# Attention computed once in query-major form, and feed-forward blocks moved behind it

## The chip, the cores and the metric

The kernel runs on one core of one Trainium2 chip. The metric is the device time of one execution in microseconds (us), the median of three runs. PE is TensorE (its weight loads, which overlap its matmuls, are listed apart as PEld), DVE is VectorE, ACT is ScalarE, POOL is GpSimd, and SP is the queue that issues every DMA.

## What is computed

Rotary attention over 4 batches of 8 heads, with 576 positions of 64 numbers, feeds two feed-forward layers over the 2304 tokens. The weights arrive as 64-bit numbers.

```python
q_rot, k_rot = rotate(q), rotate(k)                      # (4, 8, 576, 64)
scores = (1 / np.sqrt(64)) * q_rot @ k_rot.transpose(0, 1, 3, 2)
attn = np.exp(scores - scores.max(-1, keepdims=True))
attn = attn / (attn.sum(-1, keepdims=True) + 1e-09)
x = (attn @ v).transpose(0, 2, 1, 3).reshape(2304, 512)
g = s * np.maximum(x @ w_in, 0) ** 2 + b                 # w_in 512 x 2048
x = g @ w_out                                            # w_out 2048 x 512
gate, val = x @ w_gate, x @ w_val                        # 512 x 1536 each
out = (gate / (1 + np.exp(-gate)) * val) @ w_out2        # w_out2 1536 x 512
```

## The kernel before

Every operation is first put into a list with its engine, an estimated duration, a priority and the buffers that it takes and frees (`Schedule`, `op`, `dma`). `sch.run()` then plays an event model through that list and emits each engine's instructions in the order that the model found. On the chip each engine works through its own fixed order and waits on semaphores. Products of 32-bit numbers are made from a high and a low part in the format that TensorE takes at full rate: a product in a feed-forward layer is three matmuls (`mm3`, L953 to L956: high by high, high by low, low by high).

*Attention.* Heads go in 16 pairs. `prep(p)` loads q and k of a pair, rotates them (15 operations on POOL), transposes them on TensorE (9 transposes, L504), splits them into high and low parts (`qkhi`, `qklo`) and spreads these by six or seven DMAs (L540) into the operand tiles `a`, `t`, `kh` and `ac`, of which there are two sets, one for even and one for odd pairs. A set is taken for the next pair but one when the last matmul that reads it, one of the transposed scores, is done (`opb0`, `opb1`).

`head(n)` computes the scores of one head twice. The first time they are query-major (L632: 10 tiles of 128 by 288, two matmuls each), only so that DVE can take each row's maximum (L634) and, in 20 of the heads, ACT the sum of exponentials (L637). The maxima are turned into a row by a TensorE transpose and written as two extra rows into `ac`, in most heads through a DMA to memory and one back (`c_d`). The second time the scores are key-major (L762: 10 tiles, two matmuls each), with the maximum already subtracted by the extra rows. ACT takes the exponentials, which are at once the operand of the product with v. In 20 heads the exponentials are split in two and multiplied with `[vh|vl]`, the two parts of v side by side (L831, L833: 18 matmuls of 288 columns). The other 12 heads, 11 in `PLAIN` and one in `BH`, use a 32-bit matmul (L784), which the trace records as two instructions.

*Feed-forward blocks between.* `block_a(j)` takes 256 of the first 1536 tokens through half of the first layer (8 of 16 chunks of 128 hidden units). Its instructions are laid between those of the attention as fast as batches of attention are finished, and its partial sums go to memory (`p_d`). The 16 weight tiles that it needs are loaded and decoded during attention (`weight`: one 512 KB DMA into one of two `raw` buffers, L335 to L346 to turn 64 into 32 bits, L364 and L371 for high and low part).

*Feed-forward after attention.* `block_b` takes 384 tokens at a time: two full blocks, then four half blocks, to which the partial sums are added. `block_2` then takes six blocks of 384 tokens through the second layer (L954 to L956 for gate and value, L1198 to L1200 for the last product, whose matmuls have 512 columns). Only when attention has left its memory (`switch`) do the other weight tiles get their place.

PSUM has eight banks: five for scores and transposes (`t`), one for the product with v (`v`), and one each for the feed-forward blocks' hidden units (`h`) and sums (`x2`).

The two passes over the scores are these lines of `head` (L631 to L634 and L761 to L763):

```python
for y, (lh, rh) in enumerate(((a, t), (ac, kh))):
    nc.tensor.matmul(ps[:, 0:HS], lh[:, q0:q0 + 128], rh[:, c0_ + hf * HS:c0_ + (hf + 1) * HS], start=y == 0, stop=y == 1)
def mx(i=i, hf=hf):
    nc.vector.tensor_reduce(out=st["nm"][:, hf, i:i + 1], in_=st["s", i, hf], axis=AX.X, op=ALU.max, negate=True)
...
for y, (w, m) in enumerate(((t, a), (kh, ac))):
    nc.tensor.matmul(
        ps[0:kn, 0:HS], w[:, c0_ + kc * 128:c0_ + kc * 128 + kn], m[:, c0_ + qh * HS:c0_ + (qh + 1) * HS], start=y == 0, stop=y == 1
    )
```

Of the kernel before, what the change touches and what calls it, by code (L numbers as in the profile page):

```python
# [181 lines left out]
def tile_attention_moe_moe(  # L182
# [22 lines left out]
    FA = F1 // 2  # L205
# [4 lines left out]
    UA = 256  # L210
    UB = 384
    NA = 1536
    LATE, LAST = 1 << 20, 1 << 21
    PLAIN = (0, 1, 2, 3, 4, 5, 6, 9, 10, 13, 17)
    XP0 = 100
    XL0 = "dve"
    BH = (7,)
    DX = 1
    EWA = 0
    EVA = 0  # L220
    LDA = 800
    E1P = ("apaa", "ppap", "apaa", "ppap", "ppap", "rpap", "ppap", "pprp", "appa", "ppap", "apaa", "ppap", "apaa", "ppap", "apaa", "apaa", "apaa", "apaa", "apaa", "apaa", "apaa", "apaa", "apaa", "ppap", "apaa", "ppap", "aaaa", "ppap", "ppap", "ppap", "apaa", "apaa")
    MULE = "pool"
    WARM = 40
    G2P = 1
    RLD = 0
    SOFF = {5: 8, 31: -3, 25: 5, 23: 8, 21: -5, 22: 8}
    TOFF = {9: -3, 15: -8, 29: -8, 26: -8}
    A0 = 5000
    AS = 20  # L230
    AR = 1.0
    AVP = 3
    CPR = 8
    EVP = 8
    STP = 16
    FASTC = 4
    LA = 0
    WP0 = 80
    WPS = 4
    GLA = ("pool", "act", "dve")  # L240
    XLA = "dve"
    GLB = ("dve", "dve", "dve")
    PREP = 24
    PREP1 = 20

    GA = 8
# [4 lines left out]
        "raw": 2, "dec": 2, "wa": 2 * FA, "x": 2, "vr": 2, "ry": 1, "hi": 1, "vh": 3, "opb0": 1, "opb1": 1, "sm": 3, "l": 3, "cr": 1, "e": 2, "ph": 4,  # L251
        "pl": 4, "xo": 2, "tmp": 2, "rb": 1, "t": 5, "v": 1, "x2": 1, "h": 1, "xh": 2, "ya": 2, "ga": GA, "ra": 1,
# [4 lines left out]
    wa_p = ctx.enter_context(tc.tile_pool(name="wa", bufs=2 * FA))  # L257
    raw_p = ctx.enter_context(tc.tile_pool(name="raw", bufs=2))
    dec_p = ctx.enter_context(tc.tile_pool(name="dec", bufs=2))
    moa = ExitStack()  # L260
    xh_p = moa.enter_context(tc.tile_pool(name="xh", bufs=2, side="right"))
    ya_p = moa.enter_context(tc.tile_pool(name="ya", bufs=2, side="right"))
    ra_p = moa.enter_context(tc.tile_pool(name="ra", bufs=1, side="right"))
    ga_p = moa.enter_context(tc.tile_pool(name="ga", bufs=GA, side="right"))
    ps_x = ctx.enter_context(tc.tile_pool(name="ps_x", bufs=1, space=PSUM))
    ps_h = ctx.enter_context(tc.tile_pool(name="ps_h", bufs=1, space=PSUM))

# [147 lines left out]
    for g in range(G):  # L415
# [3 lines left out]
        if g == 0:  # L419
            eye_op = dma(ident, eye, 65536, -99, after=rt_op)  # L420
# [19 lines left out]
    def prep(p):  # L440
# [96 lines left out]
        if p:  # L537
# [13 lines left out]
            if p > 1:  # L551
                acs.append(sp(ac[64:66, 0:2 * S], lambda: kh[66:68], pr + 6))
# [749 lines left out]
```

## Time and profile before

| | |
|---|---|
| median of 3 runs | 1277.96 us (1275.68 to 1284.71) |
| profiled execution | 1277.72 us, its span 1275.9 us |
| PE, DVE, ACT, POOL busy | 1211.0, 738.1, 576.8, 332.5 us |
| TensorE instructions | 7236 matmuls |
| mean granted TensorE clock | 0.979 of full speed |

A busy share is the share of time in which at least one instruction of the engine was under way. Matmuls overlap each other by more than half, so that the time that one costs in a stream is read from the starts of successive ones and not from its duration. [...]

### The profile page before, as it was taken

How to read it: one execution, taken by the hardware profiler on the slowest of the kernel's cores; microseconds unless marked ns; L12 is line 12 of the kernel's file. 1: busy time of each engine (PE TensorE's matmuls, PEld its weight loads, DVE VectorE, ACT ScalarE, POOL GpSimd, SP SyncE). 2: the span in 40 equal slices, each digit the busy share in tenths (PEclk: the TensorE clock that was granted, in tenths of full speed). 3: DMA queues.
4: the chain of work that ended last, by engine and by line, in shares of the span. 5: the costliest groups of instructions: out<-in, count | busy, mean ns of one | idle time of the engine just before them, and what ended most of it. 6: DMA issues, size and time to landing. Idle time of an engine off the chain costs nothing.

```text
span 1275.9 us, 20228 instructions
## 1 busy us (share of the span) xinstructions
PE 1211.0 (95%) x7236; PEld 1123.1 (88%) x7236; DVE 738.1 (58%) x1652; ACT 576.8 (45%) x1549; POOL 332.5 (26%) x474
## 2 busy tenths in 40 slices
PE   6998798899999999999999999999999999999998
PEld 5666577698888889999999999999999999999997
DVE  6766777677888878688878846941212121121211
ACT  3655476678888888644434312431212121121111
POOL 8566556664564433211111000100000000000000
PEclk7899799999999989999999999999999999999999
DMA  6776664545543433343535522610001010010000
GB/s 138 168 177 155 178 154 99 106 106 128 137 104 89 119 82 85 101 143 118 164 118 163 191 82 65 191 33 16 35 1 50 1 50 1 1 50 1 26 1 25
DMA packets 124993, 116.56 MB, mean 91 GB/s; under 512 B 66870, under 2 KB 109128, under 8 KB 124892
## 3 DMA queue, kind: packets, MB, share of 16 engines
q1 hardware_dynamic: 124892, 115.26, 33.7%
q8 instruction: 57, 0.93, 0.3%
q14 instruction: 44, 0.36, 0.1%
HBM read 71.02 MB, written 17.55 MB: 69 GB/s over the span
## 4 chain that ended last, share of the span: by engine, by line
PE 83%; DMA 6%; DVE 6%; ACT 2%; SPq 1%; issue 1%; POOL 0%; DVEq 0%; ACTq 0%; POOLq 0%
PE hb L956 11%; PE hb L954 11%; PE hb L955 11%; PE ps_s L632 6%; PE ps_st L762 5%; PE acc L1200 4%; PE acc L1199 4%; PE acc L1198 4%; PE ps_av L784 4%; PE acc L955 4%; PE acc L954 3%; PE acc L956 3%; DMA ac<-qkhi 3%; DVE nm L634 2%; DMA ac<-kh 2%; PE ps_av L831 2%
## 5 line engine op out<-in xcount | busy, mean ns | idle before, releaser
L956 PE MATMUL hb<-xh,w 128*128 128x384 f32 x832 | 279.8, 336 | 0.0
L954 PE MATMUL hb<-xh,w 128*128 128x384 f32 x832 | 279.7, 336 | 0.0
L955 PE MATMUL hb<-xl,w 128*128 128x384 f32 x832 | 279.5, 336 | 0.0
L1228 DVE TENSOR_TENSOR si<-hb,si 128x384 f32<-128x384 f32 x72 | 40.1, 557 | 281.1 <-PE hb L956 280.7
L954 PEld LDWEIGHTS hb<-xh,w 128*128 128x128 f32 x832 | 156.2, 188 | 3.0
L955 PEld LDWEIGHTS hb<-xl,w 128*128 128x128 f32 x832 | 156.2, 188 | 3.0
L956 PEld LDWEIGHTS hb<-xh,w 128*128 128x128 f32 x832 | 156.2, 188 | 0.0
L634 DVE TENSOR_REDUCE nm<-ps_s 128x1 f32<-128x288 f32 x320 | 134.7, 449 | 36.4 <-PE ps_s L632 33.8
L371 POOL TENSOR_TENSOR w<-dec,w 128x512 fp32r<-128x512 f32 x42 | 58.5, 1393 | 273.1 <-ACT w L364 265.8
L632 PE MATMUL ps_s<-t,a 128*128 128x288 f32 x320 | 110.4, 351 | 10.2 <-DVE cr L666 4.3
L1226 ACT ACTIVATE si<-hb 128x384 f32<-128x384 f32 x72 | 35.4, 492 | 186.0 <-PE hb L956 182.9
L632 PE MATMUL ps_s<-kh,ac 128*128 128x288 f32 x320 | 96.3, 306 | 19.1 <-DMA ac<-kh 9.9
L762 PE MATMUL ps_st<-a,t 128*128 128x288 f32 (+1 forms) x320 | 104.0, 330 | 4.2 <-DVE rr L730 2.5
L1230 ACT ACTIVATE uh<-si 128x384 fp32r<-128x384 f32 x72 | 37.8, 525 | 149.2 <-DVE si L1228 149.2
L637 ACT ACTIVATE ps_s<-ps_s,nm 128x288 f32<-128x288 f32 x200 | 94.6, 474 | 12.8 <-DVE nm L634 12.1
L762 PE MATMUL ps_st<-ac,kh 128*128 128x288 f32 (+1 forms) x320 | 95.0, 302 | 2.0 <-DMA ac<-c_d 1.4
L632 PEld LDWEIGHTS ps_s<-t,a 128*128 128x128 f32 x320 | 62.6, 196 | 27.2 <-DVE cr L666 5.0
L955 PE MATMUL acc<-gl,w 128*128 128x384 f32 x256 | 85.9, 336 | 0.0
L954 PE MATMUL acc<-gh,w 128*128 128x384 f32 x256 | 85.6, 334 | 0.0
L956 PE MATMUL acc<-gh,w 128*128 128x384 f32 x256 | 85.5, 334 | 0.0
L1200 PE MATMUL acc<-w,ul 128*128 128x512 f32 x216 | 85.0, 393 | 0.0
L1199 PE MATMUL acc<-w,uh 128*128 128x512 f32 x216 | 84.8, 392 | 0.0
(134 smaller groups left out, 2856.9 us busy)
## 6 DMA issues: line engine op xcount, KB each, us to landing
raw<-in_moe_w_out_dram SPq DMA_DIRECT2D x28, 512.0 KB
raw<-in_moe_w_in_dram SPq DMA_DIRECT2D x16, 512.0 KB
raw<-in_moe_w_gate_dram SPq DMA_DIRECT2D x12, 512.0 KB
raw<-in_moe_w_val_dram SPq DMA_DIRECT2D x12, 512.0 KB
x_d<-xo SPq DMA_DIRECT2D x16, 288.0 KB
y_d<-y SPq DMA_DIRECT2D x24, 192.0 KB
xl<-y_d SPq DMA_DIRECT2D x6, 768.0 KB
out_dram<-o SPq DMA_DIRECT2D x18, 256.0 KB
```

The source lines that it names most:

```text
L371: e.tensor_tensor(out=W[key][:, 1], in0=val, in1=W[key][:, 0].bitcast(F32), op=ALU.subtract)
L632: nc.tensor.matmul(ps[:, 0:HS], lh[:, q0:q0 + 128], rh[:, c0_ + hf * HS:c0_ + (hf + 1) * HS], start=y == 0, stop=y == 1)
L634: nc.vector.tensor_reduce(out=st["nm"][:, hf, i:i + 1], in_=st["s", i, hf], axis=AX.X, op=ALU.max, negate=True)
L637: nc.scalar.activation(out=ps, in_=ps, func=AF.Exp, bias=st["nm"][:, hf, i:i + 1], accum_out=st["l"][:, hf, i:i + 1])
L762: nc.tensor.matmul(ps[0:kn, 0:HS], w[:, c0_ + kc * 128:c0_ + kc * 128 + kn], m[:, c0_ + qh * HS:c0_ + (qh + 1) * HS], start=y == 0, stop=y ...
L784: nc.tensor.matmul(st["av", qh][0:2 * D if wide else D + 1, 0:HS], vv, st["e", key][0:kn], start=kc == 0, stop=kc == 4)
L954: nc.tensor.matmul(o, lh, rh, start=first, stop=False)
L955: nc.tensor.matmul(o, lh, rl, start=False, stop=False)
L956: nc.tensor.matmul(o, ll, rh, start=False, stop=last)
L1198: nc.tensor.matmul(o, uh[:, cs], w[:, 0], start=first, stop=False)
L1199: nc.tensor.matmul(o, uh[:, cs], w[:, 1], start=False, stop=False)
L1200: nc.tensor.matmul(o, ul[:, cs], w[:, 0], start=False, stop=last)
```

## The change

Attention is rewritten by pairs of heads (`pair`). The scores are computed once, query-major, for nine tiles of 128 queries (the fifth tile holds the last 64 queries of one head and the first 64 of the other): four matmuls of 288 columns per tile, eight for the fifth. They lie in a PSUM tile of two banks, of which there are two (`s`). DVE takes the maximum of 576 columns in one instruction, and ACT the exponential of 576 columns with its sum, into a tile in SBUF (`e`, 12 buffers). TensorE then transposes the exponentials: 45 transposes of 128 columns a pair, four to a bank of `t` (3 buffers). ACT copies each bank into a high part, DVE subtracts it for the low part, and the product with `[vh|vl]` uses 512 columns (18 matmuls a pair) or, for the tile that two heads share, 64 columns (another 18). All heads go this way; the 32-bit product, the extra rows of maxima and their DMAs are gone, and the tile `ac` with its spreading DMA too. `a` is now laid out with a gap of 64 columns and filled by four DMAs of half its length, `t` by two, and `kz`, which was `kh`, by one. An operand set is taken for the next pair but one when the last scores of its pair are done.

`block_a` and its partial sums are removed: no feed-forward block is laid between the attention. After it, `block_b` takes all 2304 tokens through the full first layer in blocks of 512, 512, 512, 384 and 384, and `block_2` takes the same blocks through the second. The first block's first matmul is ordered behind the last scores (`s_turns`). 12 weight tiles are loaded during attention, the other 20 of the first layer behind `switch`. Sums use the two `s` tiles, hidden units the banks of `t` and `v`.

```diff
-    UA = 256
-    UB = 384
-    NA = 1536
+    UBS = (512, 512, 512, 384, 384)
+    WA = 12
+    WB = 20
+    NE = 12
...
             ops = []
             for s0, s1, d0 in a_pieces(0, 2 * S):
                 n = s1 - s0
+                ops.append(sp(a[0:64, d0:d0 + n], lambda s0=s0, s1=s1: st["hi"][0:64, s0:s1], s0 == 0))
+                ops.append(sp(a[64:128, d0:d0 + n], lambda s0=s0, s1=s1: st["lo"][0:64, s0:s1]))
+            ops.append(sp(t[64:128], lambda: st["hi"][64:128]))
+            ops.append(sp(t[0:64], lambda: st["lo"][64:128]))
+            ops.append(sp(kz[0:64], lambda: st["hi"][64:128]))
...
+        for u in range(NU):
+            pr = base + 10 * u
...
+                for hf in range(2):
+                    todo = [(q0, k0 + hf * HS, m) for q0, k0 in terms for m in (t, kz)]
+                    for y, (q0, k0, m) in enumerate(todo):
+                        nc.tensor.matmul(ps[:, hf * 512:hf * 512 + HS], a[:, q0:q0 + 128], m[:, k0:k0 + HS], start=y == 0, stop=y == len(todo) - 1)
+
+            def mx(u=u):
+                nc.vector.tensor_reduce(out=st["nm"][:, u:u + 1], in_=st["s", u], axis=AX.XY, op=ALU.max, negate=True)
+
+            def ex(u=u):
+                st["e", u] = e_p.tile([128, S], F32, tag="e", name="e")
+                nc.scalar.activation(
+                    out=st["e", u].rearrange("p (f n) -> p f n", f=2), in_=st["s", u], func=AF.Exp, bias=st["nm"][:, u:u + 1], accum_out=st["l"][:, u:u + 1]
+                )
+
+            o = s_prev = op("pe", t_mm(HS, 4 * len(terms)), s_mm, pr, (*main, s_prev), (s_tok, l_tok) if u == 0 else (s_tok,), (opb,))
+            in_turn(o, s_turns)
+            o = op("dve", t_dve(S), mx, pr, (o,))
+            exps[u] = op("act", t_act(S, True, 1) + 0.09, ex, pr + 1, (o,), (e_tok[u],), (s_tok,))
...
+        def unit(name, srcs, rows, pr, chain, av):
...
+            def tr():
+                ps = st["pt", name] = ps_t.tile([128, 512], F32, tag="t", name="ps_t")
+                for z, (u, k0, m) in enumerate(srcs):
+                    nc.tensor.transpose(ps[0:rows, z * 128:z * 128 + 128], st["e", u][:, k0:k0 + rows], ident)
+
+            def hi():
+                st["ph", name] = ph_p.tile([128, 512], F32R, tag="ph", name="ph")
+                nc.scalar.activation(out=st["ph", name][0:rows, 0:n], in_=st["pt", name][0:rows, 0:n], func=AF.Copy)
+
+            def lo():
+                ph = st["ph", name]
...
+                nc.vector.tensor_tensor(out=dst, in0=st["pt", name][0:rows, 0:n], in1=ph[0:rows, 0:n].bitcast(F32), op=ALU.subtract)
...
+        def product(name, out_cols, cols, o, toks, j, kcs, pr, chain, v_tok, first, stop, acq):
+
+            def av():
+                if v_tok not in st:
+                    st[v_tok] = ps_v.tile([128, 512], F32, tag="v", name="ps_av")
+                ps = st[v_tok][:, out_cols]
+                for y, (kc, c) in enumerate(zip(kcs, cols)):
+                    vv = st["vh"][j][:, kc]
+                    last = stop and y == len(kcs) - 1
+                    nc.tensor.matmul(ps, vv, st["ph", name][:, c], start=first and y == 0, stop=last and ("pl", name) not in st)
+                    if ("pl", name) in st:
+                        nc.tensor.matmul(ps, vv, st["pl", name][:, c], start=False, stop=last)
...
     for p in range(NP):
-        prep(p)
-        head(2 * p)
-        head(2 * p + 1)
-    for z in range(2 * FA):
-        weight(("out" if z % 2 else "in", z // 2), ("wa",), WP0 + WPS * z, spread_op[0][0][1][0])
+        sts[p] = prep(p)
+    for p in range(NP):
+        ends += pair(p, sts[p])
     n_att = len(sch.ops)
-    for j in range(NA // UA):
-        block_a(j)
...
+    for z in range(WA):
+        weight(("out" if z % 2 else "in", z // 2), ("wa",), WP0 + WPS * z)
+    sw = op("sp", 0.0, switch, LATE - 1, [o for o in sch.ops[:n_att] if o not in ends])
...
-                hs.append(op("pe", t_mm(n, 3), fn, prio + step * rate, (outs[kk], W_op["in", f], *hs[-1:]), (h_tok,) if kk == 0 else (),
+                hs.append(op("pe", t_mm(n, 3), fn, prio + step * rate, (outs[kk], W_op["in", f], *(hs[-1:] or s_turns[-1:])), (h_tok,) if kk == 0 else (),
```

## Rows read from the trace of the kernel before

**Rows 1.** The page's forty slices: TensorE's busy tenths and granted clock.

```profile
PE   6998798899999999999999999999999999999998
PEclk7899799999999989999999999999999999999999
```

**Rows 2.** Windows by stage: length, each engine's busy time and count, clock, DMA.

```profile
0.00:22.00 22.00, 12.78 (x101) 11.14 (x102) 9.88 (x21) 7.67 (x14) 18.39 (x35) 0.77 0.74 165
22.00:150.00 128.00, 111.54 (x593) 82.36 (x592) 94.22 (x211) 65.86 (x162) 82.87 (x112) 0.94 0.69 164
...
250.00:531.60 281.60, 262.16 (x1956) 249.46 (x1957) 226.41 (x626) 229.98 (x763) 129.49 (x209) 0.98 0.42 101
...
555.00:825.00 270.00, 269.99 (x1572) 269.30 (x1571) 212.21 (x388) 100.80 (x192) 31.70 (x22) 1.00 0.44 138
825.00:1275.90 450.90, 445.79 (x2341) 417.72 (x2340) 104.65 (x185) 91.55 (x180) 3.95 (x3) 1.00 0.07 23
```

**Rows 3.** Chain that ended last, 0 to 555 us: shares, one piece.

```profile
by line: PE ps_s L632 12.7%; PE ps_st L762 11.2%; PE ps_av L784 8.7%; DMA ac<-qkhi 6.0%; DVE nm L634 3.9%; DMA ac<-kh 3.6%; PE ps_av L831 3.5%; PE ps_av L833 3.2%; PE x2a L954 2.9%; PE h L954 2.9%; DMA c_d<-cr 2.9%; PE h L956 2.8%; PE h L95
...
381.26 6.48 DMA ac<-qkhi
```

**Rows 4.** Timeline of TensorE in the second layer: start, duration, instruction.

```profile
1262.34 0.34 PE L954 MATMUL hb<-xh,w 128*128 128x384 f32 x1
...
1266.58 0.39 PE L1198 MATMUL acc<-w,uh 128*128 128x512 f32 x1
...
1270.43 0.39 PE L1200 MATMUL acc<-w,ul 128*128 128x512 f32 x1
```

**Rows 5.** Timeline of TensorE in attention, at full clock.

```profile
300.50 0.29 PE L762 MATMUL ps_st<-a,t 128*128 128x288 f32 x1
...
302.20 0.28 PE L954 MATMUL h<-xh,w 128*128 128x256 f32 x1
...
302.55 0.29 PE L762 MATMUL ps_st<-a,t 128*64 128x288 f32 x1
...
354.55 0.91 PE L504 MATMUL pst<-ident,x 128*128 128x128 f32 x6 [1.61 <-DVE rr L730]
355.39 0.40 PE L632 MATMUL ps_s<-t,a 128*128 128x288 f32 x1
```

**Rows 6.** Timeline of TensorE at the first scores, at half clock.

```profile
21.41 0.45 PE L632 MATMUL ps_s<-kh,ac 128*128 128x288 f32 x1
...
22.37 0.45 PE L632 MATMUL ps_s<-kh,ac 128*128 128x288 f32 x1
22.61 0.84 PE L504 MATMUL pst<-ident,x 128*128 128x128 f32 x3
23.11 0.59 PE L632 MATMUL ps_s<-t,a 128*128 128x288 f32 x1
```

**Rows 7.** Timeline of DVE: nine maxima in a stream, and what follows.

```profile
200.12 3.50 DVE L634 TENSOR_REDUCE nm<-ps_s 128x1 f32<-128x288 f32 x9
203.53 0.40 DVE L1010 TENSOR_SCALAR r<-r,sv,bv 128x256 f32<-128x256 f32 x1
```

**Rows 8.** Groups by line: count, busy us, mean ns of one, idle before.

```profile
L1228 DVE TENSOR_TENSOR si<-hb,si 128x384 f32<-128x384 f32 x72 | 40.1, 557 | 281.1 <-PE hb L956 280.7
L485 POOL TENSOR_TENSOR x<-x,rt 128x384 f32<-128x384 f32 x46 | 48.3, 1050 | 0.9
L1249 ACT ACTIVATE o<-acc 128x512 f32<-128x512 f32 x12 | 7.1, 595 | 14.2 <-PE acc L1200 12.0 <-DMA out_dram<-o 2.1
L1247 DVE COPY o<-acc 128x512 f32<-128x512 f32 x6 | 4.2, 692 | 12.6 <-PE acc L1200 12.6
```

**Rows 9.** The chain, 505 to 515 us: two exponentials with their sums.

```profile
507.85 0.96 ACT ps_s L637 x4
```

**Rows 10.** Timeline of ACT: first and last of 13 streamed weight tiles.

```profile
560.33 0.63 ACT L364 ACTIVATE w<-dec 128x512 fp32r<-128x512 f32 x1 [2.49 <-DVE dec L346]
...
614.21 0.63 ACT L364 ACTIVATE w<-dec 128x512 fp32r<-128x512 f32 x1 [2.83 <-DVE dec L346]
```

More of the change, by code (lines that the diff above doesn't have):

```diff
@@ new lines, in r0, with r1, r2, r3 @@
+        def r0():
+            nc.vector.tensor_scalar(out=st["l"], in0=st["l"], scalar1=1e-9, scalar2=None, op0=ALU.add)
+        def r1():
+            nc.vector.reciprocal(out=st["l"], in_=st["l"])
+        def r2():
+            st["pr"] = ps_t.tile([128, 512], F32, tag="t", name="psr")
+            nc.tensor.transpose(st["pr"][0:NU, 0:128], st["l"], ident)
+        def r3():
+            st["rr"] = cr_p.tile([NU, 128], F32, tag="cr", name="rr")
+            nc.vector.tensor_copy(st["rr"], st["pr"][0:NU, 0:128])
@@ new lines, in pair @@
+        for j in range(2):
+            us = range(QA) if j == 0 else range(QA + 1, NU)
+            v_tok, tmp = Token("v"), Token("tmp")
+            chain = None
+            for kc in range(5):
+                pr = base + TA + TB * j + 9 * kc
+                name = (j, kc)
+                rows = 128 if kc < 4 else 64
+                o, toks = unit(name, [(u, kc * 128, 128) for u in us], rows, pr, None, None)
+                full = slice(0, 512)
+                chain = product(name, full, [full], o, toks, j, [kc], pr + AVP, chain, v_tok, kc == 0, kc == 4, kc == 0)
+            o = lower(512, (chain,), pr + 1, v_tok, tmp, j == 0)
+            evict(slice(0, 512), slice(64 * j, 64 * j + 512), j, o, pr + 1, v_tok, tmp)
@@ new lines, in pair @@
+        pr = base + TA + 2 * TB
+        o4, toks4 = unit("r", [(QA, kc * 128, 128) for kc in range(4)], 128, pr, None, None)
+        o5, toks5 = unit("rt", [(QA, 512, 128)], 64, pr + 1, None, None)
+        v_tok, tmp = Token("v"), Token("tmp")
+        chain, lasts = None, []
+        for j in range(2):
+            oc = slice(64 * j, 64 * j + 64)
+            chain = product("r", oc, [slice(128 * kc + 64 * j, 128 * kc + 64 * j + 64) for kc in range(4)], o4, toks4, j, range(4), pr + AVP, chain, v_tok, True, False, j == 0)
+            chain = product("rt", oc, [oc], o5, toks5, j, [4], pr + AVP, chain, v_tok, False, True, False)
@@ new lines, in pair @@
+        o = lower(128, (chain,), pr + AVP + 1, v_tok, tmp, False)
+        for j in range(2):
+            evict(slice(64 * j, 64 * j + 64), slice(512, S) if j == 0 else slice(0, 64), j, o, pr + AVP + 1, v_tok, tmp)
+        mul = op("pool", t_pool(S), lambda: nc.gpsimd.tensor_tensor(out=st["xo"], in0=st["xo"], in1=st["rb"], op=ALU.mult),
+                 pr + 20, (*evs, rb_op), (), (rb_tok,))
+        pp = p % (H // 2)
+        x_store[b].append(sch.dma(294912, lambda: nc.sync.dma_start(out=x_d[b][pp * 128:(pp + 1) * 128, :], in_=st["xo"]),
+                                  pr + 20, (mul,), (), (xo_tok,)))
@@ L1181, in block_2 @@
         nt = UB // 128
-        acc_toks = tuple(Token("acc") for _ in range(nt))
+        a_toks = (Token("s"), Token("s"))
+        acc_toks = (a_toks[0], a_toks[0], a_toks[1], a_toks[1])
         step = 0
@@ L1192, in fn @@
                     if first and c == 0:
-                        st["acc"] = [late["acc"].tile([128, 512], F32, tag="a", name="acc2") for _ in range(nt)]
+                        st["acc"] = []
+                        for _ in range(2):
+                            t = ps_s.tile([128, 1024], F32, tag="s", name="acc2")
+                            st["acc"] += [t[:, 0:512], t[:, 512:1024]]
                     w = W["out2", f]
```

733 lines of the change are left out of this document (203 added, 530 removed).

## The prediction, made before the change was run

> **What bounds the kernel now.** I read the page's slices first: TensorE is busy in every slice, solidly from slice 18 on, and before that with gaps in which its granted clock dips [rows 1]. So there are two kernels in one, and windows by stage separate them [rows 2]. From 555 us on TensorE is busy in 716 of 721 us at full clock: nothing but fewer or cheaper matmuls shortens that part. Before 555 us it holds attention and the early feed-forward blocks, and no engine is full: from 22 to 150 us TensorE is busy 87% and DVE 74% at a mean clock of 0.94; from 250 to 531.6 us 93% and 80%. The chain of waits says what is lost there [rows 3]: beside TensorE's own lines it holds 6.0% + 3.6% of 555 us, 53 us, in DMAs that spread a pair's operands (one piece is shown, 6.48 us), 2.9% in the row of maxima going through memory, and 3.9% in the maxima.
>
> **The feed-forward work, term by term.** Durations of matmuls overlap, so a price is the distance of starts. In the second layer 24 matmuls of 384 columns take 1266.58 − 1262.34 = 4.24 us, 0.177 each, and 17 of 512 columns take 3.85 us, 0.227 each [rows 4]. Among attention, 288 columns cost 0.131 (13 in 1.70 us) and 256 cost 0.117 (3 in 0.35 us) [rows 5].
> Before: `block_a` is 6 blocks of 8 chunks of 24 matmuls, 1152 × 0.117 = 135 us, and the rest is the 721 us from 555 on, of which the last 5 are eviction and the store; together 851 us.
> After: the first layer is 3 × 384 matmuls of 512 columns and 2 × 384 of 384: 1152 × 0.227 + 768 × 0.177 = 397 us. The second is 3 × 432 of 512, 2 × 288 of 384 and 2 × 108 of 512: 1512 × 0.227 + 576 × 0.177 = 445 us. Sum 842, take 843. Wider blocks save 8 us, no more; the fate of the change lies in attention.
>
> **What attention costs now.** 555 − 22 us of start − 135 us of `block_a` leaves 398 us for 16 pairs, 24.9 us a pair.
>
> **What a pair costs after, engine by engine.**
> TensorE: the scores are 40 matmuls of 288 columns, 5.2 us. Transposes are 45 for the exponentials and 9 for q and k; six took 0.84 us before the next matmul [rows 5], 0.14 each, and three 0.50 us at half clock [rows 6], which would be 0.083 at full clock. I take 0.11, as the ends are equally near, for 5.9 us (4.5 to 7.6). The product with v is 18 × 0.227 = 4.1 us. The 18 matmuls of 64 columns occur nowhere; between a proportional share of 288 columns (0.03) and a full such matmul (0.131) I take the 0.11 of a transpose: 2.0 us (0.5 to 2.4). Sum 17.2 us (14.3 to 19.3). The second pass over the scores and the 32-bit products that this replaces were 40 matmuls of 288 columns and more a pair, so that TensorE saves little: transposing is not much cheaper than computing again.
> DVE: nine maxima of 288 columns start to start take 3.41 us, 0.38 each [rows 7]. From 384 to 512 columns a duration grows from 557 to 692 ns [rows 8], 1.05 ns a column; so I estimate 0.68 for 576 columns, 0.615 for 512, 0.48 for 384 and 0.14 for 64. A pair has 9 maxima (6.1), 11 low parts (6.8) and a short one (0.2), evictions (2 × 0.615 + 2 × 0.14 = 1.5), three low parts of q and k (1.5) and small things (0.4): 16.5 us. Decoding 12 weights in 16 pairs adds some 1.2. Sum 17.7 us.
> ACT: two exponentials of 288 columns with their sums take 0.96 us in a stream [rows 9], so 0.48 each, and at 0.8 ns a column 0.71 for 576. A copy of 512 lasts 0.595 [rows 8], in a stream about 0.5. 9 × 0.71 + 11 × 0.5 + 1.2 for evictions + 1.4 for q and k + 0.8 for weights = 15.3 us.
> POOL: rotation at 1.05 us for 384 columns [rows 8], three times that and four halves of some 0.6, 10.4 us; splitting v, the multiply and the weights at the same 2.7 ns a column up to 6 more: at most 17.
>
> So four engines come out within 3 us of one another, DVE in front with 17.7 and TensorE beside it. How near a pair comes to 17.7 us depends on how well the fixed orders mesh. The trace has TensorE, the bound of its stages, at 0.87 and 0.93 busy [rows 2], the second with feed-forward matmuls to fill holes. I take 0.85, below both, because here two engines have to be full at once: 17.7 / 0.85 = 20.8, say 21 us. The ends are 0.95 (18.6 us) and DVE's own 0.74 of 22 to 150 us (24 us).
>
> **Where the stalls go.** The spreading DMAs keep their size (seven issues a pair on SP; one of 288 KB, that of `ac`, is gone, and two of `a` are halved into four), but the operand set is released after the last scores of its pair, not after a second pass. The next spread then has the other pair's scores, about 20 us, to land in, against pieces of about 6.5 us [rows 3]. I cost them at nothing; if SP is held up by a DMA queued in front of them (the store of 1 / sum and its broadcast, which wait for the pair's end), they are back at 53 us in the whole. The row of maxima, its transposes and its trips through memory are gone. What is late next is DVE: two `s` tiles, each held through 0.53 us of matmuls, 0.7 of maximum and 0.7 of exponential, and a maximum queued behind a low part holds up scores, exponentials and later transposes alike. `v` has one bank, and no product can start until ACT and DVE have emptied it.
>
> **The handover.** 13 weight tiles are finished 12 × 4.49 us apart [rows 10]. Before, 16 tiles had to come while the first late block ran. Now the first block (384 × 0.227 = 87 us) finds 12 and must get 20: 20 × 4.5 = 90 us, with some 8 us of head for the first. Its last chunk wants its weight at 82 us, and gets it at 91. I take a stall of 8 us, between 0 (if loading starts earlier than the block) and 20 (if it starts behind the last pair's evictions). The second layer's tiles have the last first-layer block and their own first block to come in, 36 tiles in some 165 us; no stall.
>
> **The sum.** Start until the first scores 22 (the same preparation [rows 2, 6]), 16 × 21 = 336, feed-forward 843, weights 8, last eviction and store 5: a span of 1214, and 2 outside it as in the profiled execution (1277.72 over 1275.9, which also stands within 0.3 us of the median): **1216 us**. Against before: 62 from the pairs, 8 from feed-forward, less 8 of stall. Everything but the pairs is 880, so the change breaks even at (1278 − 880) / 16 = 24.9 us a pair.
>
> **The rivals.**
> *Nearly saturated engines.* If the orders mesh at 0.95, a pair takes 18.6 us: 1178. For it: two pairs are in flight at different steps, with 12 buffers for exponentials. Against: one bank for `v`, two for scores, and no engine but TensorE passes 0.82 in the stages with attention [rows 2].
> *A latency-bound loop of scores.* DVE stays at 0.74 as from 22 to 150 us, 24 us a pair: 1264. For it: three engines follow one another in each tile and nothing fills TensorE's holes now. Against: in that stage the spreading DMAs are part of the loss.
> *TensorE at half clock.* This is the one that ends slower. While feed-forward blocks filled the holes from 250 us on, the mean clock was 0.98; in the stages without or nearly without them 0.77 and 0.94 [rows 2], after TensorE had waited. At half clock 288 columns cost 0.24 and a transpose 0.167 [rows 6]; with 512 columns at 0.43 and 64 at 0.167 a pair needs 9.6 + 9.0 + 7.7 + 3.0 = 29.3 us of TensorE, and 34 us with its waits. If half the pairs run so, a pair averages 27.5 us: 1320. It decides from 0.3 of the pairs on, where the average passes 24.9. Against: TensorE was kept at full clock through most of 22 to 150 us while it waited 13% of the time, and with 17.2 of 21 us it is about as busy here.
> [...]
>
> **How the numbers follow.** My forecast (20 to 22.5 us a pair, 1195 to 1245) has 0.54; saturated engines 0.16 (about 1178); the latency-bound loop 0.17 (1245 to 1290); half clock in a good part of the pairs 0.13 (above 1290). A measurement of this kernel cannot tell less than about 1% from no change, that is 1265 to 1291. Faster takes the first two and about half of the third: 0.79. The rest of the third is the same, 0.08. Slower 0.13. A range of 1170 to 1285 leaves out 0.05 below and some 0.14 above; it holds the bounds of the small matmuls and transposes (±2 us a pair where TensorE leads) and of the weight stall.
>
> **What the profile after would show.** Right: the last scores at about 355 us, and TensorE busy all the time behind that; DVE at some 0.85 until then, with the maximum and the low part as its two largest groups, near 750 and 690 ns in duration; no spreading DMA among the chain's first entries; clock at 1.00 but for the first 25 us; 384 matmuls of 512 columns in the first block with a gap of a few us near its end. Wrong: half-level stretches in the clock row within attention; TensorE waiting for DMA at each pair's first scores; DVE below 0.75, with waits in circles between scores, maximum and exponential; or a first block well over 100 us, its matmuls waiting for ACT's weight tiles.

## The result, and the profile after

The changed kernel takes **1243.63 us** in the median (1241.40 to 1244.78), against 1278.38 for the kernel before on the same chip: a ratio of 0.9719, with a 95% interval of 0.9681 to 0.9758. The forecast was 1216 us in a range of 1170 to 1285. The direction and the range hold; the time is 27.6 us longer than forecast.

The page of the changed kernel: span, TensorE, DVE and the granted clock in forty slices, to be laid beside [rows 1].

```profile
span 1239.6 us, 16562 instructions
...
PE   5788889998999989999999999999999999999998
...
DVE  5899989887988989334344388871311211221211
...
PEclk7999989999999999999999999999999999999999
```

Attention is now a stage of its own. It ends in slice 12 (a slice is 31 us). DVE's digits stay between 7 and 9 from slice 2 to slice 16, because behind attention DVE decodes weights beside the first feed-forward block, and then fall to 3; before, TensorE had feed-forward matmuls among attention up to slice 17. Windows by stage, cut at the first and the last maximum of the scores (columns as in [rows 2]):

```profile
0.00:22.20 22.20, 11.37 (x97) 9.96 (x97) 8.26 (x19) 6.60 (x13) 16.03 (x31) 0.80 0.70 161
22.20:364.70 342.50, 303.83 (x2024) 260.83 (x2025) 302.30 (x518) 262.93 (x587) 222.45 (x301) 0.97 0.62 147
364.70:1239.60 874.90, 860.16 (x4066) 740.94 (x4064) 383.52 (x617) 220.16 (x392) 43.86 (x29) 1.00 0.17 55
```

The middle row is the 16 pairs, but for what follows the last maximum: 342.5 us, **21.4 us a pair**. DVE is busy in 0.88 of it, TensorE in 0.89, ACT in 0.77, POOL in 0.65: as the sum had it, four engines close together with DVE and TensorE in front. The same measure of the kernel before, from its first maximum at 20.5 us to its last at 509.2, is 488.7 us, 30.5 us a pair, with 106 of the 135 us of `block_a` inside (895 of its 1138 recorded matmuls).

The groups by line in the changed kernel answer the durations that were worked out from [rows 7, 8, 9] (columns: busy us, mean ns of one, idle before and what ended it).

```profile
L582 ACT ACTIVATE e<-ps_s,nm 128x576 f32<-128x576 f32 x144 | 106.5, 740 | 29.8 <-DVE nm L578 28.3
...
L634 PE MATMUL ps_t<-ident,e 128*128 128x128 f32 (+1 forms) x720 | 107.2, 277 | 8.2 <-DVE qklo L485 4.4 <-ACT e L582 1.8 <-DVE pl L647 1.7
L578 DVE TENSOR_REDUCE nm<-ps_s 128x1 f32<-128x576 f32 x144 | 106.5, 749 | 10.8 <-PE ps_s L575 9.1
...
L647 DVE TENSOR_TENSOR pl<-ps_t,ph 128x512 fp32r<-128x512 f32 x144 | 96.9, 683 | 10.9 <-ACT ph L638 9.9
```

Maximum and low part are DVE's two largest groups in this stage, at 749 and 683 ns (foretold: near 750 and 690). TensorE's new instructions are priced by their starts, in its timeline among the pairs:

```profile
300.45 1.04 PE L634 MATMUL ps_t<-ident,e 128*128 128x128 f32 x8
301.25 0.38 PE L575 MATMUL ps_s<-t,a 128*128 128x288 f32 x1
...
302.66 0.30 PE L665 MATMUL ps_av<-ph,vh 128*128 128x64 f32 x1 [0.64 <-DVE xo L677]
...
304.69 0.38 PE L575 MATMUL ps_s<-t,a 128*128 128x288 f32 x1
```

Eight transposes take 0.80 us to the next start, 0.10 each; the 18 matmuls of 64 columns take 2.03 us, 0.11 each. Both had been set at 0.11, the second between 0.03 and 0.131 with no row of its own.

The chain of waits from 0 to 364.7 us ([rows 3] are its counterpart) shows no single owner, and the spread is still in it:

```profile
by line: PE ps_s L575 11.3%; PE ps_t L634 8.8%; DMA kz<-qkhi 8.6%; PE ps_av L665 8.4%; PE ps_av L667 6.9%; DVE nm L578 6.2%; issue 5.4%; SPq L510 3.8%; DVE pl L647 3.7%; ACT e L582 3.3%; DMA vr<-in_v_dram 3.2%; DVE qklo L485 3.2%; DVE xo L6
...
39.62 6.78 DMA kz<-qkhi
```

Two places behind the last maximum cost TensorE time. Near the end of the first feed-forward block the timeline of the changed kernel shows this:

```profile
437.39 0.50 PE L761 MATMUL hb<-xh,w 128*128 128x512 f32 x1 [0.94 <-ACT w L333]
437.41 1.28 POOL L340 TENSOR_TENSOR w<-dec,w 128x512 fp32r<-128x512 f32 x1 [5.38 <-ACT w L333]
...
437.44 1.53 DVE L824 TENSOR_SCALAR gh<-r,bv 128x512 fp32r<-128x512 f32 x1
...
438.75 0.50 PE L763 MATMUL hb<-xh,w 128*128 128x512 f32 x1 [0.63 <-POOL w L340]
...
527.78 0.49 DVE L824 TENSOR_SCALAR gh<-r,bv 128x512 fp32r<-128x512 f32 x1
```

TensorE waits for a weight's high part from ACT and then for its low part from POOL. DVE's `gh` lasts 1.53 us beside POOL's low part, and 0.49 us ninety microseconds later without it. The same pair of instructions appears in the last first-layer block, where the second layer's weights are decoded:

```profile
739.55 1.74 POOL L340 TENSOR_TENSOR w<-dec,w 128x512 fp32r<-128x512 f32 x1 [7.36 <-ACT w L333]
...
740.06 1.45 DVE L824 TENSOR_SCALAR gh<-r,bv 128x384 fp32r<-128x384 f32 x1
...
742.69 0.45 PE L762 MATMUL acc<-gl,w 128*128 128x384 f32 x1 [0.69 <-DVE gl L829]
```

### The profile page after: what moved, and what is told of

Its sections match the earlier page's. It is cut to its first block, busy times and chain, and to the rows that moved or that the text cites. A ratio compares the mean times of both kernels' runs of the same rounds, so it can differ in the third digit from the quotient of the medians.

```text
span 1239.6 us, 16562 instructions
## 1 busy us (share of the span) xinstructions
PE 1175.4 (95%) x6184; PEld 1011.7 (82%) x6184; DVE 694.1 (56%) x1150; ACT 489.7 (40%) x991; POOL 282.3 (23%) x360
## 4 chain that ended last, share of the span: by engine, by line
PE 74%; DVE 10%; DMA 7%; ACT 3%; SPq 3%; issue 2%; POOL 1%; ACTq 0%; DVEq 0%; POOLq 0%
PE hb L761 12%; PE hb L763 12%; PE hb L762 12%; PE acc L762 4%; PE acc L763 4%; PE acc L761 4%; PE acc L952 4%; PE acc L954 4%; PE acc L953 4%; PE ps_s L575 3%; PE ps_t L634 3%; PE ps_av L665 3%; DMA kz<-qkhi 3%; PE ps_av L667 2%; DVE nm L578 2%
## 5 line engine op out<-in xcount | busy, mean ns | idle before, releaser
L761 PE MATMUL hb<-xh,w 128*128 128x512 f32 (+1 forms) x800 | 296.7, 371 | 0.9 <-ACT w L333 0.9
L763 PE MATMUL hb<-xh,w 128*128 128x512 f32 (+1 forms) x800 | 296.3, 370 | 0.6 <-POOL w L340 0.6
L762 PE MATMUL hb<-xl,w 128*128 128x512 f32 (+1 forms) x800 | 295.8, 370 | 0.0
L761 PE MATMUL acc<-gh,w 128*128 128x512 f32 (+1 forms) x320 | 118.8, 371 | 3.8 <-DVE gh L824 3.8
L762 PE MATMUL acc<-gl,w 128*128 128x512 f32 (+1 forms) x320 | 119.3, 373 | 3.3 <-DVE gl L829 3.2
L575 PE MATMUL ps_s<-t,a 128*128 128x288 f32 x320 | 103.5, 340 | 18.1 <-ACT e L582 16.5
L665 PE MATMUL ps_av<-ph,vh 128*128 128x512 f32 (+1 forms) x320 | 106.8, 362 | 12.2 <-DVE xo L677 7.8
L582 ACT ACTIVATE e<-ps_s,nm 128x576 f32<-128x576 f32 x144 | 106.5, 740 | 29.8 <-DVE nm L578 28.3
L763 PE MATMUL acc<-gh,w 128*128 128x512 f32 (+1 forms) x320 | 118.2, 369 | 0.0
L638 ACT ACTIVATE ph<-ps_t 128x512 fp32r<-128x512 f32 (+1 forms) x192 | 104.1, 566 | 28.9 <-PE ps_t L634 27.7
L634 PE MATMUL ps_t<-ident,e 128*128 128x128 f32 (+1 forms) x720 | 107.2, 277 | 8.2 <-DVE qklo L485 4.4
L578 DVE TENSOR_REDUCE nm<-ps_s 128x1 f32<-128x576 f32 x144 | 106.5, 749 | 10.8 <-PE ps_s L575 9.1
L647 DVE TENSOR_TENSOR pl<-ps_t,ph 128x512 fp32r<-128x512 f32 x144 | 96.9, 683 | 10.9 <-ACT ph L638 9.9
```

Of the source, the lines that this page charges most:

```text
L575: nc.tensor.matmul(ps[:, hf * 512:hf * 512 + HS], a[:, q0:q0 + 128], m[:, k0:k0 + HS], start=y == 0, stop=y == len(todo) - 1)
L578: nc.vector.tensor_reduce(out=st["nm"][:, u:u + 1], in_=st["s", u], axis=AX.XY, op=ALU.max, negate=True)
L582: nc.scalar.activation(out=st["e", u].rearrange("p (f n) -> p f n", f=2), in_=st["s", u], func=AF.Exp, bias=st["nm"][:, u:u + 1], accum_ou ...
L634: nc.tensor.transpose(ps[0:rows, z * 128:z * 128 + 128], st["e", u][:, k0:k0 + rows], ident)
L638: nc.scalar.activation(out=st["ph", name][0:rows, 0:n], in_=st["pt", name][0:rows, 0:n], func=AF.Copy)
L647: nc.vector.tensor_tensor(out=dst, in0=st["pt", name][0:rows, 0:n], in1=ph[0:rows, 0:n].bitcast(F32), op=ALU.subtract)
```

## The experiments

Four theories were to be told apart; all concern what sets the 21.4 us of a pair. **A**, the prediction's own: DVE is in front, at 17.7 us, with TensorE just behind. **B**: the loop of one score tile (matmuls, maximum, exponential, two tiles in turn) sets the pace by its latency. **T**: TensorE is the bound. **D**: the DMAs that spread the operands, costed at nothing, hold the pairs up. Beside these stand the questions of what the un-laid feed-forward blocks were worth in the kernel before, and of what the weights cost behind attention.

All ratios are against the kernel before on the same chip, with 95% intervals. The stage is the time from the start of the first maximum of the scores to the end of the last in the profiled execution, and over 16 it is the pace of a pair.

| kernel | median us | ratio | stage us | us a pair |
|---|---|---|---|---|
| the change | 1243.63 | 0.9719 [0.9681, 0.9758] | 342.5 | 21.4 |
| e8_start (pairs untouched) | 1244.86 | 0.9712 [0.9675, 0.9749] | 348.1 | 21.8 |
| e10_low_dve (pairs untouched) | 1234.71 | 0.9657 [0.9615, 0.9699] | 346.4 | 21.6 |
| e1_spread | 1235.31 | 0.9643 [0.9613, 0.9672] | 336.9 | 21.1 |
| e2_low | 1236.37 | 0.9667 [0.9620, 0.9714] | 339.5 | 21.2 |
| e3_max | 1235.31 | 0.9655 [0.9601, 0.9708] | 339.2 | 21.2 |
| e4_scores | 1240.34 | 0.9689 [0.9650, 0.9728] | 341.7 | 21.4 |
| e7_all (low parts, maxima, scores) | 1226.79 | 0.9571 [0.9542, 0.9600] | 326.3 | 20.4 |
| e11_all_spread (e7 and spreads) | 1208.42 | 0.9427 [0.9398, 0.9455] | 311.3 | 19.5 |
| e13_all_act (e11 and ACT's high part) | 1196.80 | 0.9339 [0.9323, 0.9356] | 300.6 | 18.8 |
| e9_v2 | 1267.72 | 0.9887 [0.9851, 0.9923] | 361.7 | 22.6 |
| e12_wa14 | 1243.13 | 0.9702 [0.9679, 0.9725] | 345.6 | 21.6 |
| e5_unlaid | 1384.71 | 1.0805 [1.0769, 1.0840] | 466.5 | 29.2 |

The first three rows have the same pairs, and their stages lie between 342.5 and 348.1 us with a mean of 345.7. They come in the order of TensorE's mean granted clock in the profiled execution: 0.986 in the change, 0.983 in e10_low_dve, 0.977 in e8_start. A difference of 3 us from their mean therefore says nothing, and cuts are measured against the mean.

### One suspect at a time

**The spreading DMAs.** From the third pair on, each piece is cut to 32 columns.

```diff
+            n_sp = lambda o: o.shape[1] if p < 2 else 32
-  dma_start(out=o, in_=i())
+  dma_start(out=o[:, 0:n_sp(o)], in_=i()[:, 0:n_sp(o)])
```

> The changed kernel (1243.6 us) with the seven spreading DMAs of every pair from the third on cut to 32 columns each, so that the scores of those pairs are made of left-over operands; every issue and wait stays. The chain of waits of the changed kernel holds 7.9% of its first 400 us, 32 us, in these DMAs. Theory A (DVE's and TensorE's own work sets the pair, and the chain passes through the DMAs only because they are issued as late as they may): 1235 to 1244. Rival D (the spread is the wait that paces the pairs): 1205 to 1218.

1235.31 us, and a stage 9 us below the mean of the untouched ones. Its interval lies just below that of the change: 8 to 10 us in all, half a microsecond a pair. That is the lower end of A's range and far from D's 1205 to 1218. D is a part, and a small one while the rest stands.

**DVE's low parts**, 64 columns of 512, TensorE's work kept by reading those 64 again and again.

```diff
-  tensor_tensor(out=dst, in0=pt[0:rows, 0:n], in1=ph[0:rows, 0:n], op=subtract)
+  w = n if tail else 64
+  tensor_tensor(out=dst[:, 0:w], in0=pt[0:rows, 0:w], in1=ph[0:rows, 0:w], op=subtract)
```

> The changed kernel with DVE's low part of the exponentials computed for 64 of 512 columns, and the matmuls on it reading those 64 columns eight times, so that the low part is wrong and TensorE's work is the same: 9 times 0.47 = 4.2 us of DVE less in a pair. Theory A (DVE's total of some 17.7 us a pair is in front, TensorE's 17.2 right behind it): a pair falls from 21.8 to about 20.3 us, the run to 1215 to 1225. Rival B (the two score tiles, held through scores, maximum and exponential, pace the pair): 1235 or more, since the low part is not in that loop. Rival T (TensorE alone is the bound): 1238 to 1244.

**DVE's maxima**, over 128 scores of 576 from the second pair on.

```diff
-  tensor_reduce(out=nm[:, u:u + 1], in_=st["s", u], axis=XY, op=max)
+  tensor_reduce(out=nm[:, u:u + 1], in_=st["s", u][:, :, 0:HS if p < 1 else 64], axis=XY, op=max)
```

> The changed kernel with DVE's maximum taken over 128 of 576 columns, so that the subtracted maximum is not the row's: 9 times 0.47 = 4.2 us of DVE less in a pair, as much as with the shortened low part, but inside the loop of the score tiles. Theory A: the same 1215 to 1225 as there, since only DVE's total counts. Rival B: clearly more, 1175 to 1205, each tile being held 0.47 us less. Rival T: 1238 to 1244.

**TensorE's scores**, only the product with `kz` from the second pair on.

```diff
-  todo = [(q0, k0 + hf * HS, m) for q0, k0 in terms for m in (t, kz)]
+  todo = [... for m in ((t, kz) if p < 1 else (kz,))]
```

> The changed kernel with the cross terms of the scores left out from the second pair on (only high by high): 20 matmuls of 288 columns, 2.6 us of TensorE less in a pair. Theory A: TensorE stands right behind DVE, so 0 to 0.6 us a pair, 1233 to 1244. Rival T (TensorE, with waits, is the bound): 2.6 us a pair and more, 1195 to 1205. Rival B: the tiles are held 0.26 us less each, 1215 to 1230.

The three windows from first to last maximum, in this order:

```profile
21.70:361.20 339.50, 301.81 (x2024) 265.30 (x2025) 247.34 (x518) 262.84 (x587) 221.39 (x302) 0.95 0.63 148
```

```profile
22.30:361.50 339.20, 304.89 (x2020) 264.78 (x2021) 245.59 (x518) 260.67 (x587) 220.14 (x301) 0.95 0.63 148
```

```profile
21.60:363.30 341.70, 287.55 (x1724) 235.83 (x1725) 298.57 (x518) 261.83 (x587) 219.97 (x302) 0.92 0.62 147
```

Either cut of DVE takes some 55 us out of its busy time (302.30 to 247.34 and 245.59), and the stage is 6 us below the mean of the untouched ones and 3 us below the shortest of them, the median 7 or 8 us below that of the change, with intervals that overlap. If DVE alone set the pace, most of the 55 would show: both runs miss A's 1215 to 1225, and A falls as the prediction put it. The short low part alone would have fitted B; the maxima lie inside B's loop and should have given 1175 to 1205, so that B falls with them. The scores have 300 matmuls less, 39 us at 0.131 [rows 5], and the stage is 4 us shorter, the median 3, where T wanted 1195 to 1205: T falls too, with one reserve: TensorE's busy time fell by 16 us only, as the mean clock went from 0.97 to 0.92. What was cut came back in part as a lower granted clock.

### The cuts together

e7 has the last three edits at once, e11 adds e1's, and e13 also cuts ACT's high parts to 64 columns in the same way.

> The changed kernel with all three cuts at once, low part for 64 columns, maximum over 128 columns, scores high by high only: 8.4 us of DVE and 2.6 us of TensorE less in a pair. Alone they gave 7, 8 and 3 us over 16 pairs. Theory A2 (TensorE and DVE share the path, and each cut alone only hands it to the other): together far more than the sum of 18, a pair at 17.5 to 18.5 us with ACT's 15.3 us next, 1175 to 1195. Rival C (something that none of the cuts touches paces the pairs: the single bank for the product with v, POOL, or the fixed order): no more than the sum, 1222 to 1232.

> The three cuts together (low part for 64 columns, maximum over 128 columns, scores high by high only), which gave 1226.8 us, and the spreading DMAs cut to 32 columns as well. With the three cuts the chain of waits from 190 to 330 us holds 19.7% in the spreading DMAs and 7.6% in their issue. Theory A3 (the path is shared by four parties, TensorE, DVE and the spread among them, ACT and POOL next, so that a pair stays near 20 us until the spread goes too): a pair at 17 to 18.5 us, 1175 to 1200. Rival O (the order written out for uncut durations keeps the pace, whatever gets shorter): 1215 to 1224, as far as the spread alone gave 8 us.

> All four cuts together, which gave 1208.4 us and 19.5 us a pair, and ACT's high part of the exponentials made for 64 of 512 columns as well (the matmuls read those columns eight times): 9 times 0.37 = 3.3 us of ACT less in a pair. ACT is the one engine not cut yet, 15.3 us of work in a pair of 19.5, and DVE waits most for it. Theory A3 with ACT as the next party: a pair at 17.5 to 18.5 us, 1175 to 1192. Rival O (the order written out for uncut durations, with its queues and round trips between engines, keeps the pace): 1200 to 1208.

Their windows, again from first to last maximum, in this order:

```profile
22.40:348.70 326.30, 277.16 (x1720) 233.77 (x1721) 188.15 (x517) 258.82 (x587) 220.39 (x301) 0.91 0.65 153
```

```profile
22.20:333.50 311.30, 270.53 (x1719) 228.27 (x1720) 189.72 (x517) 258.19 (x587) 220.67 (x301) 0.93 0.39 97
```

```profile
21.60:322.20 300.60, 268.12 (x1720) 230.21 (x1721) 189.57 (x518) 212.15 (x587) 222.47 (x302) 0.93 0.40 100
```

Against the mean of 345.7 the stage of e7 is 19 us shorter, about what its three cuts gave one by one (6, 6 and 4; in the medians 17 against 7, 8 and 3), with DVE's busy time down by 114 us. This is what its rival C had written, a pace set by something outside the three cuts; A2's 1175 to 1195 is missed. Taking the spreads away then gives 15 us more in the stage and 18 in the median, where alone it had given 9 and 8. ACT's cut gives another 11 and 12. Both runs end between their two ranges. What came next at each step can be seen in the chain; here from 190 to 330 us in e7:

```profile
by line: DMA kz<-qkhi 19.7%; PE ps_av L668 10.4%; PE ps_t L634 9.6%; ACT e L582 9.0%; ACT ph L638 8.5%; PE ps_av L672 8.0%; SPq L510 7.6%; PE ps_s L575 6.3%; issue 6.3%; ACT tmp L690 4.0%; ACT qkhi L483 3.8%; DVE xo L682 2.8%; DVE qklo L485
```

and from 190 to 320 us in e13:

```profile
by line: PE ps_av L675 18.3%; PE ps_t L636 16.4%; PE ps_av L681 13.0%; PE ps_s L577 10.5%; issue 7.3%; ACT e L584 7.3%; ACT tmp L699 5.4%; DVE xo L691 2.9%; ACT qkhi L483 2.6%; SPq L512 2.4%; ACT ph L641 2.1%; PE pst L472 1.9%; DMA vr<-in_v
```

Once the engines are quicker the spread is 19.7% of the chain; once it and ACT are cut, TensorE's four lines are more than half. So none of the three resources that were cut alone (DVE, TensorE's scores, the spreads) sets the 21.4 us: alone each cut is worth 3 to 10 us, and all of them, with ACT's, 47. The reading that fits is that DVE, ACT, the spreads and TensorE are so near each other that a cut of one meets the next after a few microseconds. It is shown for the spreads, which are worth about twice as much once DVE and TensorE are cut; DVE's and TensorE's cuts only add up, and ACT was cut only last. Even with all of them cut a pair stays at 18.8 us, while DVE, ACT and POOL are busy 0.63, 0.71 and 0.74 and TensorE 0.89. Whether the rest is TensorE, with its waits and its mean clock of 0.93, or the order, which was written out for the uncut durations, these runs don't settle. POOL was not cut, and an order planned anew for the cut kernel was not tried.

### One bank moved from the transposes to the product

```diff
-  "s": 2, "t": 3, "v": 1
+  "s": 2, "t": 2, "v": 2
```

> The changed kernel with two banks for the product with v and two for the transposes (before, one and three). Rival C in its most likely form (one bank for v, emptied by ACT and DVE before the next product may start, 15 waits of TensorE for 7.8 us in all): 1222 to 1235. Theory A2: within 5 us of 1243.6, since the path only changes hands, or up to 10 more, as transposes have a bank less.

1267.72 us, 22 to 24 longer than the change (by the ratios, and by the medians), and outside both ranges. The waits of TensorE within the pairs (total us, times, longest), first of the changed kernel, then of this one:

```profile
PE ps_s L575 <- ACT e L582: 16.5, 16, 7.8
PE ps_av L665 <- DVE xo L677: 7.5, 14, 1.1
PE ps_t L634 <- DVE qklo L485: 4.4, 6, 2.3
PE ps_av L667 <- DVE pl L647: 2.8, 5, 1.2
```

```profile
PE ps_s L575 <- ACT e L582: 20.1, 19, 7.7
PE ps_av L667 <- DVE pl L647: 12.8, 37, 1.1
PE ps_t L634 <- DVE qklo L485: 9.4, 15, 1.0
PE ps_av L665 <- DVE ph L647: 5.7, 11, 0.9
```

The second `v` bank takes away the wait for the eviction (7.5 us, no longer in the list), which the prediction had named as what speaks against saturated engines. The third transpose bank is worth more: without it the wait for the low part grows from 2.8 to 12.8 us. That fewer tiles are then in flight between TensorE, ACT and DVE is the likely reason; the order is planned anew for the other banks, and the two aren't told apart. Nor is all of the loss in the pairs: their stage is 16 us above the mean, and behind its last maximum the run takes 884.6 us instead of 874.9, where the hidden units use the same banks.

### The un-laying alone

The kernel before, with no feed-forward block laid among its pairs.

```diff
-    NA = 1536
+    NA = 0
```

> The kernel before with one number changed: no tokens go through the early half blocks (NA = 0), so that the old attention runs alone and six full blocks follow it. It is the other half of the change by itself, feed-forward blocks no longer laid between, without the new attention. Theory A (the new attention pays; the old one at 24.9 us a pair beside filler keeps most of its waits when the filler goes): 16 pairs of 25 to 27 us and 22 of start, then 135 + 721 us of feed-forward: 1275 to 1315. Rival U (laying the blocks between was what cost, and taking it out is the gain): 1240 to 1255, level with the changed kernel.

1384.71 us, 103 longer than before on the same chip, and 70 above the higher of the two ranges. The window from first to last maximum of the kernel before, then that of this run, and this run's chain from 190 to 330 us:

```profile
20.50:509.20 488.70, 438.98 (x2895) 382.16 (x2896) 379.54 (x991) 350.93 (x1092) 267.72 (x401) 0.96 0.53 125
20.90:487.40 466.50, 380.14 (x1996) 300.00 (x1996) 342.72 (x879) 316.19 (x978) 242.61 (x362) 0.89 0.51 120
```

```profile
by line: DMA ac<-qkhi 19.7%; PE ps_s L632 13.4%; PE ps_st L762 8.9%; DVE nm L634 7.6%; PE ps_av L784 6.3%; ACT ps_s L637 5.7%; PE ps_av L831 4.3%; PE pst L504 4.2%; issue 4.2%; PE ps_av L833 3.7%; DVE pl L817 3.6%; DMA r_d<-rr 3.4%; SPq L54
```

Without filler a pair of the old attention takes 29.2 us, with it 30.5. The 106 us of feed-forward matmuls in that window had cost some 22 (488.7 − 466.5). They lay in time in which TensorE otherwise waits, above all for the spreads of `ac`, or is at half clock: without them the mean granted clock of the window is 0.89 instead of 0.96. The whole time says the same: the work of `block_a`, done behind attention, is 768 matmuls of 384 columns, 136 us at 0.177, and the run grew by 103, so that within attention it had cost some 33. The change is thus two large things, by the ratios: the un-laying loses 0.0805 of the time before, 103 us, and the new attention, with everything else that was changed, wins 1.0805 − 0.9719 = 0.1086 of it, 139 us. The new attention with the blocks still laid between was not run.

### Behind attention

**The first weight later**, meant to keep ACT from sitting behind its decoding at the start.

```diff
-  weight((...), ("wa",), WP0 + WPS * z)
+  weight((...), ("wa",), WP0 + WPS * z, spread_op[0][0][0])
```

> The changed kernel with the first weight's load ordered behind the first pair's operands, so that no decode stands ahead of the first exponential on ACT. In the changed kernel ACT waits 4.1 us in that decode for the weight's DMA and the third score tile waits 7.8 us for ACT. If those waits are on the path: 1235 to 1240. If the first maximum at 22 us is set by the rotation anyway: 1241 to 1245.

1244.86 us, no difference. But the edit left the wait nearly as it was: ACT still decodes ahead of the first exponential and waits 3.0 us for the weight's DMA instead of 4.1, and TensorE waits 6.7 us for the third score tile instead of 7.8. Whether that wait is on the path is not shown; for the pairs the run is one more of the change.

**Low parts of the late weights on DVE alone**, none on POOL.

```diff
-  weight(..., sw, lo_eng="dve" if z % 2 else "pool")
+  weight(..., sw, lo_eng="dve")
-  weight(..., sw, lo_eng="pool" if z % 2 else "dve")
+  weight(..., sw, lo_eng="dve")
```

> The changed kernel with the low part of every weight behind attention made on DVE, where every second one was POOL's. In the first block's last 50 us TensorE loses 10 us waiting for weight tiles and their products, and in the last first-layer block 5 more; two of DVE's conversions, gh and dec, last up to 1.53 us there while POOL works on a low part, against 0.41 and 0.37 at best. Theory P (POOL's low parts hold up DVE, which decodes the weights): DVE gets 0.6 us more for every second weight and loses the hold-ups, 1232 to 1240. Rival Q (DVE, busy 0.89 there, is the bound of the decoding by its own work): 1245 to 1252.

1234.71 us, within P's range, and the fastest kernel here that does the whole computation. Against before it is faster by 3.4%. Against the change the intervals touch (three of its four times are 1233.4 to 1235.6, one is 1245.1), but the trace says where the time went: its last maximum ends 2 us later, at 367.0, and from there it is 864.6 us to the end instead of 874.9, 10 less; e8 and the seven runs that cut only the pairs have 872.8 to 875.0 there. Groups of DVE by line, 378.5 to 500 us, first in the changed kernel, then here:

```profile
L307 DVE TENSOR_SCALAR dec<-dec 128x512 uint32<-128x512 uint32 x27 | 15.9, 589 | 2.9 <-ACT dec L304 2.6
L824 DVE TENSOR_SCALAR gh<-r,bv 128x512 fp32r<-128x512 f32 x21 | 12.2, 580 | 0.4
```

```profile
L307 DVE TENSOR_SCALAR dec<-dec 128x512 uint32<-128x512 uint32 x27 | 11.4, 422 | 0.5 <-ACT dec L304 0.2
L824 DVE TENSOR_SCALAR gh<-r,bv 128x512 fp32r<-128x512 f32 x21 | 10.1, 481 | 0.5
```

DVE took over POOL's low parts and still has `dec` and `gh` done sooner, in 422 and 481 ns instead of 589 and 580. The help from POOL cost more than it gave.

**Fourteen weights early** instead of twelve, paid for with two buffers of exponentials.

```diff
-    WA, WB, NE = 12, 20, 12
+    WA, WB, NE = 14, 18, 10
```

> The changed kernel with 14 instead of 12 weight tiles loaded during attention and 18 instead of 20 behind it; the room is taken from the exponentials, 10 buffers instead of 12. Two tiles at 4.2 us each come off the first block's wait of 10 us: 8 us less of it. The other way, two more decodes in attention (3.5 us of DVE in 16 pairs) and two buffers less for the exponentials of the next pair. If the exponentials' buffers don't matter: 1234 to 1239. If they hold up the next pair's scores: 1245 to 1275.

1243.13 us, no difference: the 8 us foretold for the two early weights did not come, and nothing was lost either. TensorE's named waits from 378.5 to 475 us fall from 6.0 to 4.5 us; its stage of pairs is as long as the mean of the untouched ones, so that two buffers of exponentials fewer cost nothing that can be seen.

## Why the prediction was right, and where it was off

**The pairs: 16 × 21 = 336, measured 342.5.** This term decided the direction, and it is 6.5 us too small. Its parts are right to a few per cent: maximum 0.68 (0.665 start to start), low part 0.615 (0.60), transposes and matmuls of 64 columns 0.11. The share, 17.7 / 21.4 = 0.83 for the foretold 0.85, is also near. The exponential came out as well: 0.71 foretold, 0.73 from start to start. No row showed its 0.8 ns a column; in the kernel before, ACT's `r` (L1000) lasts 386 ns for 256 columns and 490 for 384, 0.81 a column. The reason behind the share of 0.85 is not borne out: it was taken from "two engines have to be full at once", with DVE in front. With DVE's busy time down by 38%, and TensorE's scores cut too, a pair still took 20.4 us. DVE, TensorE, ACT and the spreads share the pace, as far as the runs tell, and that 0.85 stood for all of them is luck.

**"I cost them at nothing": the spreads.** Too kind. The operand set does come free earlier, but the single `hi`/`lo` pair of buffers and SP's queue keep the spreads in the chain at 8.6% of 364.7 us; ACT waits five times, 6.3 us, for a spread before it can write the next high part. They cost 8 or 9 us as things stand, more than the 6.5 by which the pairs were missed, and 15 to 18 once the engines are relieved. The sign foretold, no spreading DMA among the chain's first entries, was wrong.

**"What attention costs now": 24.9 us a pair.** This step took the 135 us of `block_a` off as if they had added to the pairs. e5_unlaid measured 29.2 us without them, so that they had cost about a fifth of that, and the gain of the new attention is nearly 8 us a pair, not 4. It did no harm to the total, since the sum and the break-even were made from the whole time, but who changes only one half of this kernel with that number misses the 103 us that the other half costs.

**Behind the last maximum: 843 + 8 + 5 = 856, measured 874.9.** This is the larger miss, 18.9 us. The sum stopped the pairs at their last scores: the last pair's transposes and products come after that. From 364.7 to 378.5 us TensorE starts only 24 feed-forward matmuls, 5.5 us at 0.228 each, so that 8.3 us of these 13.8 are the tail, which no term held. The matmuls are 2664 of 512 columns at 0.228 and 1344 of 384 at 0.177, 845.3 us where 843 stood: 2.3. The first block's weight stall was foretold at 8 and is 9.9, the 86.5 us from 378.5 to 465 less 336 × 0.228. The hold-up of DVE beside POOL at 741 to 780 us, where "no stall" was written, is 3.1: 39 us for 195 matmuls of 0.177 and 6 of 0.228. The end is 5.9 for 5. That makes 16.5; 2.4 I can't place. e10_low_dve won back 10 us of this stage by one edit. Beside the tail and the matmuls' own price the excess is 8.3 us, so that POOL's low parts can account for all of it and for some of the foretold stall.

**The rest.** 6.5 and 18.9 are 25.4, and 2.2 is the median above the profiled execution (1241.4, 1.8 outside its span as foretold).

**The rivals.** Saturated engines did not come about. The 18.6 us that they stood for is reached in e13 alone (18.8), with nearly everything cut and no engine busier than 0.89. The latency-bound loop had 24 us; e3_max, inside that loop, gained 6 to 8 us in 16 pairs. Half clock stayed an episode, but the clock of 1.00 that was foretold behind the first 25 us did not come either: the mean of the stage is 0.97, with four stretches at the half level (0.50, as from 174.08 us below) from 27 us on, 17 us together. By an estimate from these numbers they cost some 8 us of TensorE's work, about what the pairs were missed by; how much of that reached the time is not shown. The windows of TensorE around two of the four, with its clock behind the busy time:

```profile
170.66:174.08 3.42, 2.57 (x21) 0.93 0.28 89
174.08:177.49 3.41, 3.41 (x17) 0.50 0.01 2
...
259.41:262.82 3.41, 3.38 (x27) 0.93 0.57 149
262.82:266.24 3.42, 3.42 (x14) 0.57 0.85 186
```

and one of 60 us without any:

```profile
200.00:260.00 60.00, 54.53 (x383) 47.77 (x382) 54.62 (x96) 47.91 (x109) 42.48 (x60) 1.00 0.64 145
```

The prediction had the clock fall after waits. TensorE had waited 1.6 us ahead of the first of these, but in the 3.41 us that hold the second fall it was busy for 3.38. What it did there is the same in both, the product's 18 matmuls of 64 columns; they stand ahead of three of the four falls from 27 us on. They run in all 16 pairs, most of which see no fall, and no run leaves them out, so that they are a suspect and not a shown cause. Of the 383 instructions in the 60 us 135 are transposes of exponentials, and the clock stayed at 1.00.

## What to carry to other kernels

Before a pace is put down to the engine with the highest busy share, ask how far back the others are: here 18% off DVE's work (55 of 302 us) was worth 6 to 8 us, with TensorE as busy as DVE and ACT not far behind. Work laid into the holes of a slow stage may be cheap there (106 us of matmuls for 22), so take the stage's price without it from a run and not by subtraction; and give the tail of the last iteration a term of its own, where a new stage has to start behind it.

## What the hardware showed unexpectedly

DVE's `gh` lasted 1.53 us instead of 0.49 where a POOL instruction had started 0.03 us ahead of it (437.41 and 437.44 us): it ended 0.28 us after POOL's. At 740 us `gh` of 384 columns took 1.45 us, ending 0.22 us after POOL, and 0.41 at 770 us with no POOL low part beside it. Taking the POOL work away brought the mean of the groups of `gh` and `dec` from 580 and 589 ns to 481 and 422 in e10_low_dve. At both places DVE's instruction ends shortly after POOL's; what holds it until then these runs don't show.

In e4_scores a cut of TensorE's work was in part eaten by its own clock: with 300 matmuls less in the pairs the mean granted clock fell from 0.97 to 0.92, and the busy time by 16 us of the 39 that they take at full clock.
